# Ten outer products of tile 1's up stage in seven inner products each, with the weight sums read from three buffers

## The chip, the cores and the metric

The kernel runs on one core of a Trainium2 chip. A core has TensorE (matrix products, PE in the profile), VectorE (DVE), ScalarE (ACT), GpSimd (POOL) and SyncE (SP), each with a queue of its own that it works through in order, and DMA engines that move data between the core's memory (SBUF) and HBM. TensorE writes to PSUM; here PSUM holds four banks for products (bankA, bankB, bankC, bankE) and two areas for the attention. Transfers are started by an instruction in the queue of ScalarE or SyncE (ACTq, SPq), and whatever stands behind that instruction waits if it waits.

The metric is the device time of one execution in microseconds (us): before, the median of three runs is 1044.62 us (1042.49 to 1047.77).

## What is computed

A retention attention, whose output is the input of a SwiGLU feed-forward block; all in float32.

```python
scores = scale * np.matmul(q, k.transpose(0, 1, 3, 2))       # q, k, v: 8 x 8 heads x 576 x 64
Dmat = np.where(rel >= 0, gamma[:, None, None] ** rel[None, :, :], 0.0)
attn = np.matmul(scores * Dmat[None], v)
x = attn.transpose(0, 2, 1, 3).reshape(4608, 512)
g, val = x @ w_gate, x @ w_val                                # 512 x 1536 each
out = (g / (1 + exp(-g)) * val) @ w_out                       # 1536 x 512
```

## The kernel before

**Tiles and stages.** The 4608 tokens are worked in five tiles: tile 0 has 512 tokens, tiles 1 to 4 have 1024 each. The attention pairs of heads that a later tile needs are worked in small steps ("ticks") that are merged between the products of the tile before. Each of the tiles 1 to 4 has an up stage (gate and val products, SiLU and multiplication) and then a down stage.

**Sets.** The up stage of a tile multiplies in two levels, each a form of fast 2x2 block multiplication with seven products where eight are plain. The outer level makes seven sets, numbered 1 to 7, for each of three quarters of the hidden columns (`qd` 0 to 2); the order is `SETS = (1, 2, 6, 7, 4, 5, 3)` (line 109). A set has a 2x2 block of x and a 2x2 block of weights, for gate and val together. It is worked in one of two forms:

- *plain* (`PLAIN`, line 110): four output corners 11, 12, 21, 22, each the sum of two products, so eight slots (`whole_slot`, line 1220). A corner has one bank. When its second product is in, the bank is read once by VectorE (a 128x512 addition, `combine`), by ScalarE for set 1 (a copy), and twice by VectorE for set 5 (`whole_read`, line 1184).
- *seven inner products* (`slot`, line 1232): products 1, 5, 2, 6, 3 in the set's own slots, and 7 and 4 inside the next set's slots. Products 1, 6, 7, 4 go one after the other into one bank ("chain"), 5 and 3 into another ("side"), 2 into a third ("own"); between two products of a bank it is read (`first_read`, `second_read`), so there are seven reads instead of four. Products 1, 2, 3 use blocks of the weights as they are; products 7, 5, 6, 4 use the four *weight sums* 0, 1, 2, 3 of the set (`PLACE`, line 1043), and products 3, 5, 6, 7 use sums of x (`x_inner`, `view`).

A slot is two calls of `matmul` (gate, val) in `multiply` (line 1161); each call is two MATMUL records in the profile.

**Tile 1 before.** Tile 1 (called *busy* in the code) works all 21 sets in the plain form, 168 slots, straight from the weights in SBUF (`w_up`, the place `arena`). Meanwhile GpSimd makes for tiles 2 to 4 what they will read from HBM: for each quarter the weights of sets 5, 6, 7 and 4 (`outer_sums` in `w_sets`, eight 128x512 subtractions) and the four inner sums of all seven sets (`inner_sums`, four 128x256 subtractions for a set). Two buffers of 1024 columns hold the inner sums in turn; ScalarE's queue issues the transfers that store them (`store`, lines 1106 to 1110: the sums in one transfer of 512 KB, line 1109, the weights themselves in two of 256 KB, line 1110). A buffer is written again only when its store has landed.

**Order.** Every engine works in program order. `later(at, f)` puts an instruction ahead of slot `at`; `go` (line 1302) issues what is due, then the finished outputs that wait (`finish`, line 1171: SiLU on ScalarE into `io`, multiplication on VectorE, three slots after the output's last read), then the slot's matmuls and reads. Where a quarter begins is `begins[7 * qd]`: slots 0, 56 and 112. The first 56 slots run without ticks; over the rest six ticks are spread evenly.

```python
for i, o in enumerate(order):                       # order = (6, 4, 5, 7, 1, 2, 3)
    for j, f in enumerate(w_inner(o)):
        later(at + 8 + (13 * i + 3 * j) // 2, f)
    later(at + 8 + (13 * i + 9) // 2 + 6, *store(o, True))
```

## Time and profile before

| what | value |
|---|---|
| median of three runs | 1044.62 us |
| profiled execution, its own time | 1044.91 us |
| its span, first to last instruction | 1043.2 us |
| mean granted TensorE clock | 0.997 |
| TensorE busy | 1018.3 us (98%), 8380 matmul records |
| VectorE busy | 692.1 us (66%) |
| GpSimd busy | 551.0 us (53%) |
| ScalarE busy | 288.2 us (28%) |
| up stage of tile 1, first to last slot | 176.59 to 338.01 us of the span |

The times in the profile are counted from the first instruction. Busy shares are means over the whole span; what holds a stage is read from that stage. In the timeline, a line gives start, length, engine, line of the kernel, operation, output and inputs, and how often it follows itself; in brackets stands how long the engine had been idle before it, and what ended that. Matmuls overlap a little, so the time of a group of them is read from one start to the next.

### The profile page before, as it was taken

To read this page: it belongs to the slowest core of one execution; us is meant where nothing else is said; L and a number is where in the kernel's file an instruction comes from. 1 tells how busy PE (TensorE), PEld (TensorE's weight loads), DVE (VectorE), ACT (ScalarE), POOL (GpSimd) and SP (SyncE) were. 2 spreads that over 40 slices of the span, in tenths; PEclk is the share of its full clock that TensorE was granted. 3 is DMA by queue.
4 is the path that set the end of the run, shared out by engine and by line. 5 is a ranking of instruction groups with operands and counts; after the bars stand their busy time and mean duration, and the time that the engine had idled before them with its cause. 6 is when DMAs were issued, how large, how long until landed. Compare 5 with 4: busy or idle time off the path is not lost. (4 is left out here: it accounts for less than half of the span.)

```text
span 1043.2 us, 21372 instructions
## 1 busy us (share of the span) xinstructions
PE 1018.3 (98%) x8380; PEld 834.0 (80%) x8380; DVE 692.1 (66%) x1182; ACT 288.2 (28%) x638; POOL 551.0 (53%) x586
## 2 busy tenths in 40 slices
PE   6999999999999999999999999999999999999998
PEld 5655555888788888878888887888888888888887
DVE  4488883675857855875768777857576448566744
ACT  4466532131332321123332111133230012333110
POOL 3402263884635206854657237775582497566615
PEclk9999999999999999999999999999999999999999
DMA  9999887679485886756558767544454444445552
GB/s 241 253 273 240 213 226 252 204 190 253 134 244 156 224 240 198 198 170 172 177 157 242 202 169 203 168 148 142 142 190 152 154 157 150 169 141 176 185 159 96
DMA packets 292364, 197.13 MB, mean 189 GB/s; under 512 B 212968, under 2 KB 251112, under 8 KB 292264
## 3 DMA queue, kind: packets, MB, share of 16 engines
q10 hardware_dynamic: 58960, 121.12, 35.3%
q1 hardware_dynamic: 232664, 74.25, 29.9%
q8 instruction: 66, 1.08, 0.4%
q0 software_dynamic: 640, 0.39, 0.2%
...
## 5 line engine op out<-in xcount | busy, mean ns | idle before, releaser
L1041 POOL TENSOR_TENSOR rest<-rest 128x512 f32<-128x512 f32 (+1 forms) x147 | 155.6, 1073 | 158.6 <-DVE rest L1041 118.9
L1178 POOL TENSOR_TENSOR arena<-rest,io 128x256 f32<-128x256 f32 x144 | 105.4, 744 | 70.8 <-ACT io L1177 70.4
L1177 ACT ACTIVATE io<-rest 128x256 f32<-128x256 f32 x192 | 79.4, 417 | 225.1 <-DVE rest L1041 121.4
L1041 DVE TENSOR_TENSOR rest<-bankA,rest 128x512 f32<-128x512 f32 x100 | 67.7, 686 | 63.2 <-PE bankA L1163 46.2
L1163 PE MATMUL bankE<-rest,arena 128*128 128x256 f32 x424 | 108.0, 380 | 1.3 <-DVE rest L1041 1.2
L1163 PE MATMUL bankB<-rest,arena 128*128 128x256 f32 x416 | 106.4, 381 | 0.2
L1163 PE MATMUL bankA<-rest,arena 128*128 128x256 f32 x392 | 99.9, 381 | 1.4 <-DVE rest L1041 1.2
L1041 DVE TENSOR_TENSOR rest<-bankE,rest 128x512 f32<-128x512 f32 x108 | 73.0, 685 | 41.4 <-PE bankE L1163 23.8
L1041 DVE TENSOR_TENSOR rest<-bankC,rest 128x512 f32<-128x512 f32 x100 | 67.8, 685 | 44.0 <-PE bankC L1163 22.5
L1163 PE MATMUL bankC<-rest,arena 128*128 128x256 f32 x372 | 94.7, 381 | 0.6 <-DVE rest L1041 0.5
L1041 DVE TENSOR_TENSOR rest<-bankB,rest 128x512 f32<-128x512 f32 x101 | 68.7, 686 | 38.2 <-PE bankB L1163 25.0
L1163 PEld LDWEIGHTS bankE<-rest,arena 128*128 128x128 f32 x424 | 79.9, 190 | 14.1 <-DVE rest L1041 2.2
L1163 PEld LDWEIGHTS bankB<-rest,arena 128*128 128x128 f32 x416 | 78.2, 190 | 12.3 <-DVE rest L1041 1.1
L1163 PEld LDWEIGHTS bankA<-rest,arena 128*128 128x128 f32 x392 | 73.8, 190 | 13.6 <-DVE rest L1041 1.8
L1163 PEld LDWEIGHTS bankC<-rest,arena 128*128 128x128 f32 x372 | 69.8, 190 | 12.0 <-DVE rest L1041 2.5
L886 POOL TENSOR_TENSOR rest<-rest 128x256 f32<-128x256 f32 x43 | 35.4, 845 | 67.0 <-DVE rest L407 35.4
L1342 PE MATMUL bankE<-arena 128*128 128x256 f32 x264 | 61.0, 381 | 0.0
L1342 PE MATMUL bankC<-arena 128*128 128x256 f32 x264 | 60.8, 380 | 0.0
L1041 POOL TENSOR_TENSOR rest<-arena 128x256 f32<-128x256 f32 x42 | 31.5, 770 | 51.5 <-DMA up<-rest 51.5
L1342 PE MATMUL bankA<-arena 128*128 128x256 f32 x240 | 55.4, 380 | 1.8 <-POOL arena L886 1.8
L1342 PEld LDWEIGHTS bankC<-arena 128*128 128x128 f32 x264 | 50.0, 190 | 6.9
L1342 PEld LDWEIGHTS bankE<-arena 128*128 128x128 f32 x264 | 49.8, 190 | 6.9
...
## 6 DMA issues: line engine op xcount, KB each, us to landing
...
```

Source lines behind the costliest of these rows:

```text
L886: eng.tensor_tensor(out=dst, in0=srcs[0], in1=srcs[1], op=ALU.add if op[0] == "add" else ALU.subtract)
L1041: eng.tensor_tensor(out=out, in0=a, in1=b, op=ALU.add if sign > 0 else ALU.subtract)
L1163: m = nc.tensor.matmul(b[:, g * TB : (g + 1) * TB], w[:, g], x, start=(opens and g == 0), stop=True, skip_group_check=True)
L1177: nc.scalar.activation(out=s, in_=src[:, 0:TB], func=AF.Silu)
L1178: (nc.vector if busy else nc.gpsimd).tensor_tensor(out=hid[:, qd, 2 * H + h, 2 * T + t], in0=src[:, TB : 2 * TB], in1=s, op=ALU.mult)
L1342: nc.tensor.matmul(b[:, m * TB : (m + 1) * TB], lhs[:, qd, ts(m, P)], w[:, qd], start=(opens and qd == 0 and m == 0), stop=(qd == NQ - 1), ...
```

## The change

In tile 1, four sets of the seven in quarters 1 and 2 (6, 7, 4, 3) and two in quarter 0 (4, 3), ten in all, are worked in seven inner products instead of eight plain ones; sets 1, 2 and 5, and 6 and 7 of quarter 0, stay plain. That takes these parts:

- TensorE reads the weight sums for these sets from the buffers that GpSimd makes them in (`weights_of`: `new[o][:, :, at - 4]`). There are three buffers (`blocks`): 0 is in `rest`, 1 and 2 lie at the end of `arena`. Buffer 1 serves sets 6, 2, 5, buffer 2 serves 1, 4, and buffer 0 serves 7, 3.
- GpSimd's order in a quarter is another one: the outer sums of sets 5 and 6, the inner sums of 6, the outer sums of 7, the inner sums of 1, the outer sums of 4, and then the inner sums of 4, 7, 2, 5, 3 (in quarters 1 and 2 those of 7 ahead of 4). The stores of the sums stand at other slots: eight slots after the first sum of the set, for set 2 four.
- GpSimd also makes the inner sums of x for sets 4, 6, 3 and 7 (`x_inner`, sixteen 128x256 operations), in quarter 0.
- The first reads of sets 6, 7 and 4 in quarters 1 and 2 go by a ScalarE copy and a GpSimd addition, as they do in the later tiles (corner 12, and corner 22 of set 6, by VectorE).
- All sets share the four places of `ends`; a finished output that still waits is issued before its place is written again (`clear`). Corner 21 of set 4 has a place of its own. Corner 11 of set 5 is finished six slots on instead of three where the set before was in seven products.
- The operands of the first down steps are fetched at slots 45, 46 and 47 of quarter 2 instead of slots 120, 124 and 128.

Quarters now begin at slots 0, 52 and 104, and there are 158 slots. For each set the slots at which it starts within quarter 0 are 1: 0, 2: 8, 6: 16, 7: 24, 4: 32, 5: 37 and 3: 47; products 7 and 4 of set 4 stand at slots 39 and 43, those of set 3 at slots 2 and 6 of the next quarter.

```diff
--- before.py
+++ after.py
@@ -107,7 +107,7 @@
 
 
 SETS = (1, 2, 6, 7, 4, 5, 3)
-PLAIN = {(1, qd, o) for qd in range(3) for o in SETS}
+PLAIN = {(1, qd, o) for qd in range(3) for o in ((1, 2, 6, 7, 5) if qd == 0 else (1, 2, 5))}
 
 
 def terms(text):
@@ -1052,7 +1052,7 @@
         spots += [rest[:, sum_at + 1024 + TB * i : sum_at + 1024 + TB * (i + 1)] for i in range(2)]
         spots += [rest[:, dn_at + 4096 + TB * i : dn_at + 4096 + TB * (i + 1)] for i in range(12)]
         spots += [operands[:, 5376 + TB * i : 5376 + TB * (i + 1)] for i in range(3)]
-        new = {o: spots[3 * m : 3 * m + 3] for m, o in enumerate((1, 2, 7, 4, 5, 3, 6))}
+        new = {o: spots[3 * m : 3 * m + 3] for m, o in enumerate((1, 2, 7, 4, 6, 3, 5) if n == 1 else (1, 2, 7, 4, 5, 3, 6))}
         aside = new[3][2]
 
         def outer_sums(o, eng):
@@ -1083,13 +1083,15 @@
         first = x_inner(1, p) + x_outer(5, p) + x_outer(6, p)
         return first + x_outer(3, p) + x_inner(2, p) + x_outer(7, p) if n + 1 == NTILE else first
 
+    extra_at = lambda a, n: arena[:, 4 * QW + a : 4 * QW + a + n]
+
     def w_sets(qd):
 
         up = lambda n, k: w_up[:, qd, :, 2 * n : 2 * n + 2, k, :]
         sets = {1: up(0, 0), 2: up(0, 1), 7: up(1, 0), 3: up(1, 1), 5: hid[:, qd, 2:4, 0:2], 6: hid[:, qd, 0:2, 2:4], 4: hid[:, qd, 2:4, 2:4]}
-        new = [rest[:, a : a + 1024].rearrange("p (g j x) -> p g j x", g=2, j=4) for a in (x0_at + 1024, sum_at)]
+        blocks = (rest[:, x0_at + 1024 : x0_at + 2048], extra_at(1536, 1024), extra_at(0, 1024))
+        new = {o: blocks[b].rearrange("p (g j x) -> p g j x", g=2, j=4) for o, b in {6: 1, 1: 2, 7: 0, 4: 2, 2: 1, 5: 1, 3: 0}.items()}
         queue = nc.scalar
-        order = (6, 4, 5, 7, 1, 2, 3)
 
         def outer_sums(o):
             out, a, b = {5: (5, 7, 1), 6: (6, 3, 5), 7: (7, 3, 7), 4: (4, 2, 6)}[o]
@@ -1097,7 +1099,7 @@
 
         def inner_sums(o):
             z = lambda k, m: sets[o][:, :, m, k * P : (k + 1) * P]
-            to = lambda j: new[order.index(o) % 2][:, :, j]
+            to = lambda j: new[o][:, :, j]
             return [lambda: combine(nc.gpsimd, to(1), z(0, 1), z(0, 0), -1),
                     lambda: combine(nc.gpsimd, to(0), z(1, 1), z(0, 1), -1),
                     lambda: combine(nc.gpsimd, to(2), z(1, 1), to(1), -1),
@@ -1106,10 +1108,10 @@
         def store(o, new_ones):
             dst = up_sets[qd][SETS.index(o)].rearrange("p (g x) -> p g x", g=2)
             if new_ones:
-                return [lambda: queue.dma_start(out=dst[:, :, 512:1024], in_=new[order.index(o) % 2].rearrange("p g j x -> p g (j x)"))]
+                return [lambda: queue.dma_start(out=dst[:, :, 512:1024], in_=new[o].rearrange("p g j x -> p g (j x)"))]
             return [lambda m=m: queue.dma_start(out=dst[:, :, TB * (1 - m) : TB * (2 - m)], in_=sets[o][:, :, m]) for m in range(2)]
 
-        return sets, order, outer_sums, inner_sums, store
+        return sets, new, outer_sums, inner_sums, store
 
     def up_stage(n):
 
@@ -1125,7 +1127,7 @@
             held, ends, keep = place(0, 1, 2, 3), [place(4, 5, 6, 7)] * 2, place(8, 9, 10, 11)
         else:
             held, ends, keep = place(5, 6, 7, 10), [place(1, 3, 11, 8), place(0, 9, 2, 4)], None
-        number = {2: 0, 4: 1, 5: 0, 3: 1}
+        number = {2: 0, 4: 0, 5: 0, 3: 0} if busy else {2: 0, 4: 1, 5: 0, 3: 1}
         free = [banks[b] for b in rested] + ([inner[:, 0], outer[:, 0]] if n + 1 == NTILE else [])
         taken = {}
         waiting, after = [], {}
@@ -1143,6 +1145,8 @@
 
         def to(k, c):
             o = seq[k][1]
+            if busy and o == 4 and c == 21:
+                return rest[:, sum_at + 1024 : sum_at + 1536]
             return held[c] if o in (1, 6) else kept(k, c) if o == 7 else ends[number[o]][c]
 
         def addend(k, c):
@@ -1151,9 +1155,9 @@
         def weights_of(k):
             qd, o = seq[k]
             if busy:
-                sets = w_sets(qd)[0]
+                sets, new, *_ = w_sets(qd)
                 spot = [(kk, m) for m in (1, 0) for kk in range(2)]
-                return lambda at: sets[o][:, :, spot[at][1], spot[at][0] * P : (spot[at][0] + 1) * P]
+                return lambda at: sets[o][:, :, spot[at][1], spot[at][0] * P : (spot[at][0] + 1) * P] if at < 4 else new[o][:, :, at - 4]
             _, _, _, lo, width = fetches[base + k]
             w = operands[:, lo : lo + width].rearrange("p (g i x) -> p g i x", g=2, x=P)
             return lambda at: w[:, :, at if plain[k] else at - 1]
@@ -1179,10 +1183,18 @@
 
         def made(k, c, at):
             if seq[k][1] in final:
-                waiting.append((at + 3, k, c))
+                late = plain[k] and not plain[k - 1] and seq[k][1] == 5 and c == 11
+                waiting.append((at + (6 if late else 3), k, c))
+
+        def clear(k, c):
+            o = seq[k][1]
+            for e in [e for e in waiting if o in final and e[1] != k and e[2] == c and number[seq[e[1]][1]] == number[o]]:
+                waiting.remove(e)
+                finish(*e[1:])
 
         def whole_read(k, c, bank, at):
             o = seq[k][1]
+            clear(k, c)
             if o == 1:
                 nc.scalar.copy(out=to(k, c), in_=bank)
             elif o == 5:
@@ -1195,17 +1207,18 @@
         def first_read(k, c, bank):
             qd, o = seq[k]
             dst = to(k, c)
+            clear(k, c)
             if o == 1:
                 nc.scalar.copy(out=dst, in_=bank)
-            elif o == 5 and c != 12:
+            elif o == 5 and c != 12 and not busy:
                 nc.scalar.copy(out=dst, in_=bank)
                 combine(nc.gpsimd, held[c], held[c], dst, 1)
                 combine(nc.gpsimd, dst, dst, kept(k, c), 1)
             elif o == 5:
                 combine(nc.vector, held[c], bank, held[c], 1)
                 combine(nc.vector, dst, bank, kept(k, c), 1)
-            elif qd > 0 and o != 3 and c != 12:
-                t = ends[0 if o == 4 else 1][c]
+            elif qd > 0 and o != 3 and c != 12 and not (busy and (o, c) == (6, 22)):
+                t = dst if busy and o == 4 else ends[0 if o == 4 else 1][c]
                 nc.scalar.copy(out=t, in_=bank)
                 combine(nc.gpsimd, dst, t, addend(k, c), 1)
             else:
@@ -1286,15 +1299,19 @@
         else:
             for i, f in enumerate(x_outer(5, nc.vector) + x_outer(6, nc.vector) + x_outer(7, nc.vector) + x_outer(3, nc.vector)):
                 later(i if i < 4 else 2 * i + 2, f)
+            for o, at in {4: 16, 6: 32, 3: 36, 7: 47}.items():
+                for i, f in enumerate(x_inner(o, nc.gpsimd)):
+                    later(at + i, f)
             for qd in range(NQ):
                 at = begins[len(SETS) * qd]
-                _, order, w_outer, w_inner, store = w_sets(qd)
-                for i, f in enumerate([f for o in (5, 6, 7, 4) for f in w_outer(o)]):
-                    later(at + i, f)
-                for i, o in enumerate(order):
+                _, _, w_outer, w_inner, store = w_sets(qd)
+                for o, start in {5: 0, 6: 2, 7: 8, 4: 14}.items():
+                    for i, f in enumerate(w_outer(o)):
+                        later(at + start + i, f)
+                for o, start in {6: 4, 1: 10, 7: 24 if qd == 0 else 14, 4: 20, 2: 29, 5: 34, 3: 38}.items():
                     for j, f in enumerate(w_inner(o)):
-                        later(at + 8 + (13 * i + 3 * j) // 2, f)
-                    later(at + 8 + (13 * i + 9) // 2 + 6, *store(o, True))
+                        later(at + start + j, f)
+                    later(at + start + (4 if o == 2 else 8), *store(o, True))
                 for i, o in enumerate((1, 2, 6, 7, 4, 5, 3)):
                     for j, f in enumerate(store(o, False)):
                         later(at + 3 + 5 * i + 2 * j, f)
@@ -1309,7 +1326,7 @@
             after_tick()
             if at % (2 if busy else 3) == 1:
                 part_on()
-            if busy and at in (120, 124, 128):
+            if busy and at - begins[2 * len(SETS)] in (45, 46, 47):
                 fetch_one()
             if at + 1 == len(slots):
                 while waiting:
```

## The prediction

> **What bounds the kernel now.** I read the page's busy shares first, then the up stage of tile 1 by stretches (its quarters begin at 176.6, 225 and 273), then each engine's timeline in it.
>
> ```profile
> PE 1018.3 (98%) x8380; PEld 834.0 (80%) x8380; DVE 692.1 (66%) x1182; ACT 288.2 (28%) x638; POOL 551.0 (53%) x586
> 176.60:225.00 48.40, 48.37 (x224) 42.28 (x223) 30.77 (x45) 9.27 (x21) 35.34 (x38) 1.00 0.73 212
> 225.00:273.00 48.00, 48.00 (x410) 42.01 (x409) 29.30 (x56) 13.60 (x33) 28.59 (x36) 1.00 0.69 193
> 273.00:325.00 52.00, 49.90 (x597) 43.11 (x596) 30.79 (x59) 15.30 (x40) 24.61 (x28) 0.97 0.82 216
> ```
>
> In the last three rows the columns are length, then TensorE, weight loads, VectorE, ScalarE and GpSimd. TensorE is filled, so a matmul less is time less as long as nothing else takes the place; VectorE and GpSimd have a third of the stage free. The pitch of TensorE, and the one hole of the stage that counts:
>
> ```profile
> 190.40 1.89 PE L1163 MATMUL bankA<-rest,arena 128*128 128x256 f32 x8
> 192.13 1.89 PE L1163 MATMUL bankB<-rest,arena 128*128 128x256 f32 x8
> ...
> 279.40 0.52 PE L573 MATMUL inner<-qT,kT 64*64 64x64 f32 x21
> 282.02 0.35 PE L573 MATMUL inner<-qT,kT 64*64 64x64 f32 x9 [2.10 <-issue]
> 282.30 2.63 PE L1163 MATMUL bankA<-x_odd,arena 128*128 128x256 f32 x8
> 284.72 2.98 PE L1163 MATMUL bankB<-x_odd,arena 128*128 128x256 f32 x8
> 287.54 1.89 PE L1163 MATMUL bankC<-x_odd,arena 128*128 128x256 f32 x8
> ```
>
> Eight records take 192.13 - 190.40 = 1.73 us, so a slot of four takes 0.864 us; slot s of quarter 0 is due at 176.59 + 0.864 s. After a hole of 2.10 us two groups of eight take 5.24 us instead of 3.46 (the clock was halved): a hole of that size costs 1.8 us more than itself. GpSimd and ScalarE in quarter 0:
>
> ```profile
> 181.23 10.94 POOL L1041 TENSOR_TENSOR arena<-arena 128x512 f32<-128x512 f32 x8 [15.75 <-DMA out_dram<-arena]
> 192.13 2.04 POOL L1041 TENSOR_TENSOR rest<-arena 128x256 f32<-128x256 f32 x2
> 194.13 2.11 POOL L1041 TENSOR_TENSOR rest<-arena,rest 128x256 f32<-128x256 f32 x2
> 196.21 1.40 POOL L1041 TENSOR_TENSOR rest<-arena 128x256 f32<-128x256 f32 x2
> 197.57 1.59 POOL L1041 TENSOR_TENSOR rest<-arena,rest 128x256 f32<-128x256 f32 x2
> ...
> 196.27 0.52 ACTq L1109 DMA_DIRECT2D up<-rest  x1
> ...
> 197.51 0.42 ACT L1177 ACTIVATE io<-rest 128x256 f32<-128x256 f32 x1 [5.42 <-POOL rest L1041]
> ...
> 197.96 0.62 DVE L1178 TENSOR_TENSOR arena<-rest,io 128x256 f32<-128x256 f32 x1 [1.71 <-ACT io L1177]
> ```
>
> GpSimd starts at 181.23, held by tile 0's output; eight outer and eight inner sums are done at 197.57 + 1.59 = 199.2, four inner sums taking 3.0. The last three lines are the chain that I look for after the change: a store in ScalarE's queue waits for GpSimd's sums, a SiLU behind it waits 5.42 us, and VectorE stands behind its multiplication for 1.71 us with reads of banks queued. Here TensorE has banks enough not to notice.
>
> **What is removed.** Ten sets lose one slot each of eight: 10 x 0.864 = 8.6 us of TensorE. It has to come off the end, unless TensorE waits.
>
> **What is added.** Thirty bank reads; 16 sums of x on GpSimd (16 x 0.75 = 12 us, in quarter 0); ten copies on ScalarE and additions on GpSimd in quarters 1 and 2 (a 128x512 addition there is 1.37 by the row above); and waits of TensorE for sums just made. Seven reads with two slots or so between two products of one bank also leave VectorE less room to be late: a plain corner's bank is wanted again three corners (5 us) on, a chain or side bank three slots (2.6 us) on. The later fetch of the down operands (slots 45 to 47 of quarter 2, six to eight slots or 5 to 7 us ahead of the down stage) I cost at nothing, since such a fetch lands in 4.4 us by the page's issue list; if ScalarE issues it late, TensorE waits for the difference, 0 to 3 us, which goes into the range.
>
> **Quarter 0, GpSimd's clock.** Up to the sums of set 1 and the outer sums of set 4 GpSimd has the same sixteen operations as above, in another order: 199.2. Then x of set 4: 202.2; sums of 4: 205.2 (needed at slot 33, 205.1: nothing); sums of 7: 208.2; sums of 2 with one x operation between: 211.9. The store of set 2's sums stands at slot 33 of ScalarE's queue and so goes out at 211.9, with two weight stores of 0.63 behind it, then the SiLU of set 4's corner 11 (0.42): 214.1. VectorE's multiplication for it, at slot 37 (due 208.6), ends at 214.7. Behind it on VectorE: two reads of set 5's corner 11 (0.6 each, two take 1.29), a multiplication (0.6), the read of set 4's corner 22: 217.1. TensorE's product 4 of set 4, slot 43, goes into that bank and is due at 213.7. **First stall: 3.4 us**; slot 48 is now due at 221.4.
>
> The store of set 2 lands 3.3 us after its issue (median of its row), at 215.2, and only then may GpSimd write set 5's sums into the same buffer; with the x operations between it has seven to do: 220.4, and the first sum of set 3 at 221.9, all four at 224.9. Product 5 of set 3 (slot 48) waits 0.6. The store of set 5's sums (slot 42) has held ScalarE until 220.4, with four SiLUs behind it; four multiplications bring VectorE to 223.9, then two reads of corner 21 to 225.1: slot 49 waits 2.2. Two more reads, one multiplication that stands behind the store of set 3's sums (224.9 + 0.6 + 0.4 + 0.6), and the read of set 3's first product end at 227.5: slot 50 waits 1.5, slot 51 0.3. **Second stall: 4.6 us.** Quarter 0 gives back 8.0 of the 8.6. Ends: with GpSimd at the pace that it has where VectorE rests (1.28 for a large sum, alone at 272.88; 1.42 for two small ones at 199.40) the sixteen operations take 15.9 us instead of 18.0, and both stalls lose about 2: 4; with landings of 6.5 us, the longest of these stores' rows, 11.
>
> **Quarters 1 and 2, VectorE from set 5 to set 3.** Fifteen slots are 13.0 us of TensorE; a tick falls into them in both quarters (2.26 us, from 258.66 to 260.92). VectorE has in them 15 reads x 0.61 = 9.2, eight multiplications x 0.65 = 5.2, and the tick's own 4.0 (mask 0.6, states 2.0, two transpositions 1.4): 18.4 against 15.3. In the trace of before the same set 5 with a tick keeps VectorE busy from 265.14 to 281.79 and its last read (280.31) comes 2.6 us after its bank is full; plain sets follow and hide it. Now set 3 follows in seven products. I take the 3.1 with a little of the lag that no longer fits: **3.5 us in each quarter, 7.0.** The multiplications are the unsure term:
>
> ```profile
> L1178 DVE TENSOR_TENSOR arena<-rest,io 128x256 f32<-128x256 f32 x44 | 29.8, 678 | 7.2 <-ACT io L1177 7.2
> ```
>
> They mean 678 ns here, but 0.41 where GpSimd rests and 0.98 where it works: 1.1 us at the one end, 6 at the other, for each quarter; I take the mean since GpSimd makes sums all through this stretch. In quarters 1 and 2 GpSimd itself has 8 x 1.3 + 28 x 0.75 + 5 x 1.37 = 38 us for 52 slots and three ticks (some 51 us): no stall of its own in the likeliest case.
>
> **Sum.** -8.6 + 8.0 + 7.0 = +6.4 us against the profiled execution's 1044.9, which stands 0.3 over the median. The hole at 282.02 (2.10 + 1.8) may not come back in another program, and the first stall of 3.4 may halve the clock as that hole did (+1.8); I set these against each other. 1044.6 + 6.4 = 1051.0.
>
> The Trainium skill ("TensorE: Matmul & The Clock Gate", Part 1: The HAM clock gate) has the clock halved after an idle window of about 3.4 us. By that rule neither the 2.10 hole nor most of my stalls would cost anything beyond themselves, and the sum would stay 1051; by this case's row each stall of 2 us adds 1.8, and it would be 1053 to 1055. The row at 282.30 speaks against taking the rule as a threshold.
>
> **Rivals.**
> - *Faster: the lag never reaches TensorE.* The place is ScalarE's queue at slots 33 and 42. If GpSimd is done with set 2's sums 3.5 us earlier than I have it, the SiLU behind the store is in time, and with VectorE's lag held by the banks 2 us of stalls remain: 1044.6 - 8.6 + 2 = 1038. For it: no stall in this stage before although ScalarE was held 5.42 and 9.3 us. Against: GpSimd's start at 181.23 and its pace leave at most 2 us.
> - *A wash: quarter 0 as above, quarters 1 and 2 without stalls*, since banks absorb VectorE's 3.1: -8.6 + 8.0, 1044.
> - *Much slower: stores land late in quarters 1 and 2.* The sums of set 4 wait for the store of set 1's in the same buffer, and behind them in GpSimd's queue stand the additions of sets 7 and 4 that VectorE's second reads need. The waits for such stores before:
>
> ```profile
> POOL rest L1041 <- DMA up<-rest: 51.5, 13, 11.2
> ```
>
>  Four microseconds a wait on average and 11.2 at most, with nothing urgent behind them then. At 5 us more a quarter: 1061. It decides once a store lands over 4 us behind its slot.
>
> **How the numbers follow.** Likeliest (both kinds of stall) 0.45, its own range 1046 to 1056; faster 0.16; a wash 0.22; much slower 0.17. Range: from 1040 (between the faster case and the wash) to 1062. About 0.5% (5.2 us) is what a measurement of this kernel can tell from no change: slower than 1049.8 are the last rival and nine tenths of the likeliest, 0.58; within 0.5% the wash and a little of the likeliest, 0.25; faster 0.17.
>
> **What would show it.** TensorE's records of this stage fall by 80. Right: holes of TensorE near slots 43 and 48 to 51, put down to VectorE or GpSimd; SiLUs late behind the sums' stores; holes at set 3 of quarters 1 and 2. The steps are wrong if the stage has no holes over 0.5 us (then 8.6 us are gained), if set 2's sums end before 209, or if the holes sit at sets 7 and 4 of the later quarters. The whole is wrong if a later stage gives time back or takes it.

## The result and the profile after

Over six runs of each the kernel after takes 1055.24 us (median; 1052.82 to 1058.71) and the kernel before 1044.92 us (1039.45 to 1047.77): a ratio of 1.0107, 95% interval 1.0073 to 1.0140. It is slower by about 1%, 10.3 us by the medians; the forecast was 1051.0, so the sign holds and the time lies in the range that was given, 1040 to 1062, and the sum was 4 us short. The profiled execution took 1055.56 us (span 1053.8, mean granted clock 0.990; before 1044.91, 1043.2 and 0.997).

The line numbers move a little: TensorE's products are line 1167 now (1163 before), the stores of the sums 1111 and of the weights 1112, the SiLU 1181, its multiplication 1182. The page's busy shares of the kernel after:

```profile
PE 1016.7 (96%) x8340; PEld 828.3 (79%) x8340; DVE 698.4 (66%) x1203; ACT 292.9 (28%) x648; POOL 573.1 (54%) x612
```

TensorE has 40 records fewer (8380 before), which is ten slots of four, and is busy 1.6 us less, not 8.6. The up stage of tile 1 tells most of why. Here it is by its quarters (columns as in the prediction: length, then TensorE, weight loads, VectorE, ScalarE and GpSimd with their instructions, the granted clock, DMA):

```profile
174.60:232.50 57.90, 49.20 (x210) 40.51 (x209) 30.90 (x47) 7.90 (x18) 47.26 (x55) 0.95 0.65 193
232.50:290.10 57.60, 52.55 (x413) 44.54 (x412) 41.00 (x73) 18.48 (x43) 37.12 (x43) 0.94 0.64 177
290.10:350.50 60.40, 57.25 (x625) 48.67 (x624) 43.72 (x85) 21.50 (x53) 40.01 (x42) 0.96 0.77 208
```

The stage takes 175.9 us against 161.4 before (quarters 48.6, 57.1, 55.7), though it has ten slots fewer: the removed slots are gone (8.6 us), and 23 us of new loss stand against them. That is 14.5 us more, where the two executions differ by 10.6: the kernel after came to this stage 2.0 us earlier (174.6 and 176.6 us of the span) and needed 1.9 us less behind it (703.3 and 705.2). Both parts differ from execution to execution: over the profiles of this document the stage begins at 171.5 to 183.8 us, and what follows it takes 702.8 to 706.1. Whether any of the 3.9 us comes from the change is not shown. So the whole loss lies in this stage, and the stage shows it better than the time of a single execution. TensorE's waits over the stage in the kernel after, by what ended them (total, times, longest):

```profile
PE bankC L1167 <- DVE rest L1041: 4.6, 3, 2.3
PE bankB L1167 <- DVE rest L1041: 4.4, 3, 2.9
PE bankA L1167 <- DVE rest L1041: 3.8, 3, 1.9
PE bankE L1167 <- DVE rest L1041: 2.7, 3, 1.2
PE bankA L1167 <- POOL rest L1041: 1.4, 1, 1.4
```

That is 16.9 us; before it was one wait of 2.1 for "issue" and one of 0.4 for VectorE. Nearly all of it is a bank that VectorE has not read yet. For quarter 0, here are TensorE, then ScalarE, VectorE and GpSimd in the timeline of the kernel after:

```profile
216.40 1.10 PE L1167 MATMUL bankA<-x_odd,arena 128*128 128x256 f32 x4 [1.94 <-DVE rest L1041]
...
222.31 1.13 PE L1167 MATMUL bankA<-rest 128*128 128x256 f32 x4 [1.35 <-POOL rest L1041]
226.39 1.88 PE L1167 MATMUL bankB<-rest,arena 128*128 128x256 f32 x4 [2.95 <-DVE rest L1041]
228.92 1.62 PE L1167 MATMUL bankC<-rest 128*128 128x256 f32 x3 [0.66 <-DVE rest L1041]
...
210.82 0.52 ACTq L1111 DMA_DIRECT2D up<-arena  x1
211.38 1.71 ACTq L1112 DMA_DIRECT2D up<-arena  x2
213.19 0.72 ACT L1181 ACTIVATE io<-rest 128x256 f32<-128x256 f32 x2 [15.37 <-DMA kn<-in_k_dram]
220.92 0.52 ACTq L1111 DMA_DIRECT2D up<-arena  x1
221.54 1.34 ACT L1181 ACTIVATE io<-rest 128x256 f32<-128x256 f32 x4 [7.63 <-POOL arena L1041]
...
213.70 0.42 DVE L1182 TENSOR_TENSOR arena<-rest,io 128x256 f32<-128x256 f32 x1 [3.68 <-ACT io L1181]
...
222.05 3.09 DVE L1182 TENSOR_TENSOR arena<-rest,io 128x256 f32<-128x256 f32 x4 [3.81 <-ACT io L1181]
225.06 1.28 DVE L1041 TENSOR_TENSOR rest<-bankB,rest 128x512 f32<-128x512 f32 x2
...
216.05 0.73 POOL L1041 TENSOR_TENSOR arena<-arena 128x256 f32<-128x256 f32 x1 [3.89 <-DMA up<-arena]
```

Read from below: the store of set 2's sums goes out at 210.82, and only when it has landed, at 216.05, does GpSimd write set 5's sums; the next store, 220.92, waits for these. Each time the SiLUs stand in ScalarE's queue behind a store that waits for GpSimd (213.19, 221.54), VectorE waits for them for 3.68 and 3.81 us, and the bank reads are behind that. (The bracket at 213.19 names an old transfer: issuing a store isn't counted as busy. What ScalarE stood at is the store just above.) In the quarters behind, this is set 5 to set 3 of quarter 1, VectorE and then TensorE:

```profile
274.32 1.45 DVE L1182 TENSOR_TENSOR arena<-rest,io 128x256 f32<-128x256 f32 x1 [1.63 <-ACT io L1181]
...
279.94 1.42 DVE L1182 TENSOR_TENSOR arena<-rest,io 128x256 f32<-128x256 f32 x4
281.28 1.28 DVE L1041 TENSOR_TENSOR rest<-bankB,rest 128x512 f32<-128x512 f32 x2
...
276.43 1.13 PE L1167 MATMUL bankC<-x_odd,arena 128*128 128x256 f32 x4 [2.34 <-DVE rest L1041]
...
278.67 3.16 PE L1167 MATMUL bankA<-rest,arena 128*128 128x256 f32 x8
...
285.50 1.10 PE L1167 MATMUL bankE<-rest 128*128 128x256 f32 x4 [1.07 <-DVE rest L1041]
288.24 2.08 PE L1167 MATMUL bankC<-rest,arena 128*128 128x256 f32 x4 [1.64 <-DVE rest L1041]
```

VectorE works without a pause from 274.32 to 289.4, TensorE waits three times for it, and after the wait of 2.34 eight records take 3.00 us (278.67 to 281.67) where 1.73 is usual. The granted clock (the last column but two) in the stretches behind such waits:

```profile
226.60:233.40 6.80, 6.14 (x15) 4.38 (x15) 5.18 (x10) 1.08 (x3) 6.80 (x7) 0.50 0.39 111
277.80:281.20 3.40, 3.40 (x9) 2.65 (x9) 3.33 (x10) 0.83 (x2) 0.00 (x0) 0.50 0.06 22
288.10:291.50 3.40, 3.26 (x8) 2.63 (x9) 2.31 (x5) 0.42 (x1) 1.82 (x2) 0.50 0.80 129
346.10:349.50 3.40, 3.26 (x8) 2.64 (x9) 2.30 (x5) 0.78 (x2) 2.76 (x2) 0.50 0.57 93
214.50:222.00 7.50, 4.55 (x20) 3.72 (x20) 3.64 (x7) 0.46 (x2) 5.95 (x9) 1.00 0.72 160
```

Half clock for 17 us of the stage, worth 8.5 us of TensorE's work at most (before: one stretch of 3.4 us at 283.5). That is why TensorE is as busy in the stage as before (159.0 and 158.9 us) with 8.6 us of products less: the 13.6 us of half clock that are new make up for 6.8 of it. The last row is the wait of 1.94 at slot 43, after which the clock stayed whole.

To compare the runs I use one number for a quarter: its *loss*, the sum over its slots of what each takes above 0.8635 us, where that is over 0.15. The ticks' own work is in it: 10.7 us in quarters 1 and 2 together, before and after alike. Each row is one profiled execution; the ratios are over all runs, each against the kernel before on the same chip. Five of the runs, e1, e3, e4, f3 and g5, compute the same as the kernel after. The others multiply wrong operands in places, as is told with each; they serve to show what holds the time and are no kernels to use.

| kernel | loss of quarters 0, 1, 2 (us) | up stage (us) | ratio to before, 95% interval |
|---|---|---|---|
| before | 0.2, 8.3, 6.9 | 161.4 | 1 |
| after | 12.6, 12.4, 13.5 | 175.9 | 1.0107 [1.0073, 1.0140] |
| e1_sums_store_on_sync | 17.1, 17.4, 22.3 | 194.3 | 1.0324 [1.0273, 1.0374] |
| e2_fourth_buffer | 9.1, 11.3, 13.7 | 171.5 | 1.0090 [1.0063, 1.0118] |
| e3_ticks_moved | 12.1, 8.7, 13.9 | 172.6 | 1.0083 [1.0060, 1.0106] |
| e4_kept_warm | 12.5, 11.3, 14.4 | 175.9 | 1.0102 [1.0062, 1.0142] |
| f1_late_stores | 4.1, 11.1, 11.7 | 164.7 | 1.0085 [1.0060, 1.0111] |
| f2_sums_in_time | 5.5, 14.2, 11.6 | 169.1 | 1.0074 [1.0050, 1.0098] |
| f3_mult_on_gpsimd | 11.2, 6.0, 8.0 | 162.5 | 1.0019 [0.9993, 1.0045] |
| f4_all | 3.0, 5.7, 10.2 | 156.8 | 0.9999 [0.9972, 1.0027] |
| g1_order_and_mult | 2.5, 9.3, 8.0 | 157.4 | 0.9984 [0.9961, 1.0007] |
| g2_with_ticks | 2.6, 9.6, 12.3 | 162.2 | 1.0021 [0.9995, 1.0048] |
| g3_order_and_mult | 4.5, 6.4, 8.0 | 156.4 | 0.9955 [0.9927, 0.9982] |
| g5_order_and_mult | 2.7, 11.8, 8.5 | 160.2 | 0.9987 [0.9959, 1.0016] |

One thing bears on quarter 0 that no edit set. GpSimd stands for 16 to 19 us before its first sums of the stage, and counted from the stage's first slot it begins them at another time in each execution: 6.1 us in the kernel after, 3.7 in e2, 4.1 in f1, 8.4 in e4. Where it begins later, whatever waits for its sums is later.

### The profile page after: what moved, and what is told of

The parts are those of the page before. It is cut to its first block, busy times and chain, and to the rows that moved or that the text cites. A ratio compares the mean times of both kernels' runs of the same rounds, so it can differ in the third digit from the quotient of the medians.

```text
span 1053.8 us, 21402 instructions
## 1 busy us (share of the span) xinstructions
PE 1016.7 (96%) x8340; PEld 828.3 (79%) x8340; DVE 698.4 (66%) x1203; ACT 292.9 (28%) x648; POOL 573.1 (54%) x612
## 5 line engine op out<-in xcount | busy, mean ns | idle before, releaser
L1041 POOL TENSOR_TENSOR rest<-rest 128x512 f32<-128x512 f32 (+1 forms) x165 | 174.4, 1071 | 173.2 <-DVE rest L1041 119.6
L1167 PE MATMUL bankC<-rest,arena 128*128 128x256 f32 x412 | 106.7, 383 | 2.6 <-DVE rest L1041 2.4
L1041 DVE TENSOR_TENSOR rest<-bankC,rest 128x512 f32<-128x512 f32 x115 | 77.8, 685 | 43.3 <-PE bankC L1167 21.9
L1041 POOL TENSOR_TENSOR arena<-arena 128x256 f32<-128x256 f32 (+1 forms) x84 | 75.9, 925 | 39.5 <-ACT rest L1199 16.2
L1167 PE MATMUL bankA<-rest,arena 128*128 128x256 f32 x352 | 92.8, 388 | 0.6 <-DVE rest L1041 0.5
L1167 PEld LDWEIGHTS bankC<-rest,arena 128*128 128x128 f32 x412 | 78.1, 191 | 14.8 <-DVE rest L1041 3.0
L1167 PEld LDWEIGHTS bankE<-rest,arena 128*128 128x128 f32 x396 | 74.9, 191 | 14.2 <-DVE rest L1041 3.5
L1167 PEld LDWEIGHTS bankA<-rest,arena 128*128 128x128 f32 x352 | 67.5, 194 | 12.5 <-DVE rest L1041 2.5
L1359 PE MATMUL bankA<-arena 128*128 128x256 f32 x264 | 60.8, 380 | 0.0
L1359 PE MATMUL bankB<-arena 128*128 128x256 f32 x240 | 55.4, 380 | 1.8 <-POOL arena L886 1.8
L1359 PEld LDWEIGHTS bankA<-arena 128*128 128x128 f32 x264 | 50.0, 190 | 6.8
```

Of the source, the lines that this page charges most:

```text
L1041: eng.tensor_tensor(out=out, in0=a, in1=b, op=ALU.add if sign > 0 else ALU.subtract)
L1167: m = nc.tensor.matmul(b[:, g * TB : (g + 1) * TB], w[:, g], x, start=(opens and g == 0), stop=True, skip_group_check=True)
L1359: nc.tensor.matmul(b[:, m * TB : (m + 1) * TB], lhs[:, qd, ts(m, P)], w[:, qd], start=(opens and qd == 0 and m == 0), stop=(qd == NQ - 1), ...
```

## Experiments on quarter 0, the ticks and the clock

All of them start from the kernel after. **The stores of the sums on SyncE's queue**, so that ScalarE's SiLUs stand behind none of them:

```diff
 def store(o, new_ones):
     if new_ones:
-        return [lambda: queue.dma_start(out=dst[:, :, 512:1024], ...)]
+        return [lambda: nc.sync.dma_start(out=dst[:, :, 512:1024], ...)]
```

> One edit: the stores of the inner weight sums are issued by SyncE's queue instead of ScalarE's. Theory S (ScalarE stands at a store until GpSimd has made the sums, the SiLUs behind it are late, VectorE stands at their multiplications and does not free banks): in quarter 0 the holes near 194, 198, 214, 223 and 228 us (0.39, 1.26, 1.94, 2.95, 0.66) go, and one hole at the first sum of set 3 stays, 2 to 5 us, since GpSimd is as late as before; the half clock of 6.8 us after 226 shrinks to 3.4 or goes; 5 to 9 us less than the changed kernel (1046 to 1050, ratio to the kernel before about 1.003). Rival (GpSimd's lateness alone sets when set 3 can go on, ScalarE only follows it): the holes move together into one at set 3 of quarter 0 and the time stays within 2 us of 1055.

Measured: 1078.53 us, the slowest of all. The waits of GpSimd and of SyncE's queue in this kernel's stage (total, times, longest):

```profile
POOL arena L1041 <- DMA up<-arena: 46.2, 6, 10.7
...
SPq L1111 <- POOL arena L1041: 49.3, 7, 11.0
```

A store now stands in a queue with the attention's loads (line 282, which wait for VectorE), goes out late and lands late; GpSimd, which may not write the buffer before, waits 46.2 us instead of 10.5, and TensorE twice over 6 us for sums (6.73 at 202.1, 6.42 at 224.0). The holes at 194 and 198 us are gone, as theory S had it. So the run does not show that ScalarE's queue was innocent: it shows that the wait is bound to the store and goes where the store goes, and that three buffers leave a store no time to be late.

**A fourth buffer for set 5's sums**, so that GpSimd needn't wait for the landing of set 2's store:

```diff
-blocks = (rest[:, x0_at + 1024 : x0_at + 2048], extra_at(1536, 1024), extra_at(0, 1024))
+blocks = (..., rest[:, sum_at : sum_at + 1024])
-{6: 1, 1: 2, 7: 0, 4: 2, 2: 1, 5: 1, 3: 0}
+{6: 1, 1: 2, 7: 0, 4: 2, 2: 1, 5: 3, 3: 0}
```

The place is taken by sums of x of sets 3 and 6, which set 5's sums overwrite, here and in f1, f2 and f4: some products of tile 1 then have other operands, and GpSimd waits for TensorE's reads there.

> One edit: the sums of set 5 are made in a fourth buffer (1024 columns of rest at sum_at) instead of in buffer 1 behind set 2's sums. Theory B (GpSimd waits for the store of set 2, 3.89 us in quarter 0, and everything up to set 3's sums is late by that): the wait goes, the first sum of set 3 is there at about 218.5 instead of 222.3, the store of set 5 goes out near 217 instead of 220.9; the holes at 220.96, 223.44 and 228.26 (5.0 us together) shrink to 1 to 2 us, the one at 214.46 (1.94, behind the store of set 2's sums) stays; with the half clock of 6.8 us gone 5 to 7 us less, 1048 to 1050. Rival (VectorE has simply too much to do from set 5 to set 3, as in the later quarters): the holes at slots 49 to 51 stay at 3 us or more, and the time is 1052 to 1055.

Measured: 1053.34 us over eight executions, one of which took 2134 us (1052.77 without it); the ratio, 1.0090, lies within the interval of the kernel after. TensorE in this kernel at slots 43 and 49 to 50, and ScalarE's queue ahead of slot 49:

```profile
218.06 1.10 PE L1167 MATMUL bankA<-x_odd,arena 128*128 128x256 f32 x4 [2.66 <-DVE rest L1041]
...
226.26 1.26 PE L1167 MATMUL bankB<-rest,arena 128*128 128x256 f32 x4 [2.77 <-DVE rest L1041]
228.53 2.04 PE L1167 MATMUL bankC<-rest 128*128 128x256 f32 x4 [1.01 <-DVE rest L1041]
...
220.78 0.55 ACTq L1111 DMA_DIRECT2D up<-rest  x1
221.44 1.34 ACT L1181 ACTIVATE io<-rest 128x256 f32<-128x256 f32 x4 [6.51 <-POOL rest L1041]
```

The wait for the sum itself (1.35 at 220.96 in the kernel after) is gone, the one of 2.95 behind it is still 2.77. But the run does not take away what it was to take away: the store of set 5's sums goes out at 220.78 instead of near 217, though the sums are ready at 218.70, and hardly earlier than in the kernel after (220.92). It seems to wait for a sum of x (ended at 220.75) that goes to the same place. The four SiLUs behind it come at 221.44 as before (221.54), and VectorE waits 2.05 us for them. So this run shows that the lateness of set 3's sum is not what holds slot 49; whether the store in ScalarE's queue does, f1 below tells. Of the 3.5 us that quarter 0 loses less here, 2.1 are at slots 21 to 25, where no store was moved: GpSimd began earlier in this execution.

**The ticks of quarters 1 and 2 at other slots**, out of set 5 to set 3: they go in ahead of the slots 56 + (0, 10, 22, 51, 61, 74).

> One edit: the six attention ticks of tile 1's up stage stand at slots 56, 66, 78, 107, 117 and 130 instead of 56, 73, 90, 107, 124 and 141, so that none falls into sets 5 and 3 of quarters 1 and 2. Theory V (VectorE is overloaded there by 18.4 us of work in 15.3 us because of the tick): the holes of quarters 1 and 2 (2.34, 1.07, 1.64, 1.75, 1.23: 8.0 us) shrink to 2 us or less in all, and with them three of the half clock stretches (10.2 us, 5.1 us lost): 7 to 11 us less, 1044 to 1048. Rival (ScalarE held by the stores makes VectorE late there too, tick or not): the holes of these quarters stay above 5 us, and the time is within 3 us of 1055.

Measured: 1051.48 us, ratio 1.0083: 3.8 us less than the kernel after by the medians, where 7 to 11 were expected, and the intervals overlap. In the profile the holes of these quarters sum to 6.4 us instead of 8.0, and 3.4 us of their 10.2 at half clock are left. Without the ticks' own work quarter 1's loss falls from 8.8 to 5.1; at sets 5 and 3 it falls from 8.3 to 3.1, and 1.4 are new at slots 75 and 79. Quarter 2's is 6.8 instead of 6.4: at set 3 it falls from 5.5 to 4.2, and 1.9 are new at slots 124 to 127, as in every run with the ticks moved (f4, g2). So the tick was most of what quarter 1 lost there and a quarter of what quarter 2 lost there, and part of it only moves.

**TensorE kept busy over the holes of quarter 0** by small products into a PSUM area that nobody reads then:

```diff
+for _ in range({43: 8, 48: 4, 49: 12}.get(at, 0) if busy else 0):
+    nc.tensor.matmul(outer[:, 1, 0:P], ident, ident, start=True, stop=True, skip_group_check=True)
```

> One edit that adds work: 8, 4 and 12 small matmul calls (128x128 of the identity by itself, into a part of PSUM that the attention does not use in quarter 0) ahead of slots 43, 48 and 49 of quarter 0, about 0.2 us each, to fill the holes of 1.94, 1.35 and 2.95 us. Theory C (the holes themselves make the clock halve, which costs half of the stretch on top): the 6.8 us of half clock after 226 us go, the slots of sets 3 and 1 run at 0.86 us again, and the time is 3 us less, about 1052, although 24 calls are added. Rival (the clock is halved by something else, or the waits behind are VectorE's anyway and swallow it): no change, or longer by what the calls take beyond the holes, 1055 to 1057.

Measured: 1054.24 us. TensorE in this kernel (line 1325 is the filler):

```profile
222.58 2.84 PE L1325 MATMUL outer<-ident 128*128 128x128 f32 x24
...
227.75 1.10 PE L1167 MATMUL bankC<-rest 128*128 128x256 f32 x4 [1.41 <-DVE rest L1041]
```

The clock stays whole in quarter 0 (1.00, where the kernel after has 0.95 there), and the quarter is no shorter: 58.0 us against 57.9, loss 12.5 against 12.6. But the sum hides two things. Slot 50, which waited 0.66 behind slow products, now waits 1.41 behind fast ones: there a faster TensorE only comes earlier to the next bank that is not read. Behind it nothing waits, and slots 50 to 52 lose 0.2 us instead of 2.3. Against that this execution has a hole of 1.8 us at 189 that the kernel after hasn't: GpSimd began 8.4 us after the first slot, and VectorE waited 5.16 us for a SiLU. So of the 3.4 us that 6.8 us at half clock can cost, some 2 were gained and 0.75 were swallowed by VectorE's lateness; four executions can't tell 2 us from nothing.

**The stores later in ScalarE's queue**, with the fourth buffer, so that they stand behind the SiLUs (quarter 0: set 6 at slot 19, 1 at 19, 7 at 32, 4 at 28, 2 at 45, 5 at 50, 3 at 55; in the others set 6 at 12, 1 at 18, 7 at 22, in quarter 2 set 2 at 38), and **the sums of set 3 ahead of those of set 5 as well**:

```diff
-later(at + start + (4 if o == 2 else 8), *store(o, True))
+later(at + when[o], *store(o, True))                # f1, f2
-{4: 16, 6: 32, 3: 36, 7: 47}                        # sums of x
+{4: 16, 3: 32, 6: 43, 7: 47}                        # f2
-2: 29, 5: 34, 3: 38
+2: 29, 3: 35, 5: 39                                 # f2
```

> Set 5's sums in a fourth buffer, and the stores of the sums stay in ScalarE's queue but stand where no SiLU that is due waits behind them (quarter 0: sets 6 and 1 at slot 19, 2 at 45, 5 at 50, 3 at 55). GpSimd's order is that of the changed kernel. Theory S (ScalarE held by stores): the time that quarter 0's slots lose beyond 0.86 us each, 12.6 us in the changed kernel, falls to 4 or less, what stays being the first sum of set 3 that comes late (slot 48, 2 to 3 us); 1046 to 1049. Rival (VectorE's amount of work from set 5 to set 3): quarter 0 still loses 8 us or more, near slots 48 to 51, and the time is 1052 to 1054.

> As the run with late stores, and GpSimd makes the sums of set 3 (and of its x) ahead of those of set 5, which TensorE does not read in tile 1. Theory S and B together: quarter 0 loses 1.5 us or less beyond its slots, and 1 to 3 us less in quarters 1 and 2, 1044 to 1047, about the kernel before. If quarter 0 still loses over 4 us with the first sum of set 3 in time, neither the stores nor the sums were its cause, and VectorE's work is.

Measured: 1052.01 us for both, beside 1043.36 for before. TensorE in f1 at slots 49 and 50, and at the end of quarter 2; then that end in the kernel after:

```profile
222.60 1.13 PE L1167 MATMUL bankB<-rest,arena 128*128 128x256 f32 x4 [0.35 <-DVE rest L1041]
225.14 1.10 PE L1167 MATMUL bankC<-rest 128*128 128x256 f32 x4 [1.41 <-DVE rest L1041]
...
337.38 1.10 PE L1167 MATMUL bankA<-rest 128*128 128x256 f32 x4 [1.75 <-DVE rest L1041]
339.71 1.13 PE L1167 MATMUL bankE<-rest,arena 128*128 128x256 f32 x4 [1.23 <-DVE rest L1041]
```

```profile
343.90 1.10 PE L1167 MATMUL bankA<-rest 128*128 128x256 f32 x4 [1.75 <-DVE rest L1041]
346.24 2.07 PE L1167 MATMUL bankE<-rest,arena 128*128 128x256 f32 x4 [1.23 <-DVE rest L1041]
```

f1 differs from e2 by the places of the stores alone, and GpSimd begins at nearly the same time in both. Slot 49 waits 0.35 instead of 2.77, and quarter 0's loss falls from 9.1 to 4.1 (f2: 5.5): the store in ScalarE's queue, with the SiLUs behind it, is what held slot 49 in e2, and the same rows (221.54, 222.05, 226.39) stand in the kernel after. Over all runs f1 is not faster than e2 all the same (1.0085 against 1.0090). f1's profiled execution took 1048.40, 3.6 less than its median, so its row flatters it. With quarters 1 and 2 as they are, this order is worth 1 to 2 us by the ratios, which the intervals can't tell from nothing. The stores of quarters 1 and 2 were moved too, and these quarters lose 11.1 and 11.7 instead of 11.3 and 13.7.

The last four lines settle another point. The same two waits, 1.75 and 1.23, were followed by half clock in the kernel after (2.07 us for four records) and by whole clock in f1 (1.13). From the first of the two slots to the end of the stage f1 takes 5.4 us, the kernel after 6.6, and e2, which has the same two waits and 6.8 us at half clock, 7.6. So at this place 3.4 us at half clock cost 1.3 us, and 6.8 cost 2.3.

## Experiments on VectorE's load, and a better order

**The multiplications of sets 4 and 5 on GpSimd in quarters 1 and 2**, and nothing else:

```diff
 def finish(k, c):
-    (nc.vector if busy else nc.gpsimd).tensor_tensor(out=hid[...], in0=..., in1=s, op=ALU.mult)
+    (nc.vector if busy and not (qd > 0 and o in (4, 5)) else nc.gpsimd).tensor_tensor(...)
```

> One edit to the changed kernel: the multiplications that finish sets 4 and 5 in quarters 1 and 2 are made by GpSimd instead of VectorE (sixteen of 0.4 to 1.4 us). Theory V (from set 5 to set 3 VectorE has more work than the slots have time): the 8.8 and 6.4 us that quarters 1 and 2 lose beyond slots and ticks fall to 4 and 3 or less, and the time by 6 to 9 us with the clock, 1046 to 1049; quarter 0 is as it was. Rival (what these quarters lose comes from ScalarE's and GpSimd's lateness): they lose as much as now or more, since GpSimd gets 6 us more to do in each: 1054 to 1060.

Measured: 1044.60 us, ratio 1.0019. One condition takes 16 multiplications from VectorE and gets back 0.9% of the time. Quarters 1 and 2 of this kernel, and the moved operation in them (duration in ns, least, median, most):

```profile
231.50:282.60 51.10, 49.58 (x413) 42.76 (x412) 36.48 (x65) 18.06 (x43) 40.53 (x49) 0.99 0.68 193
282.60:337.70 55.10, 54.84 (x626) 47.17 (x626) 41.05 (x76) 21.65 (x54) 44.21 (x51) 1.00 0.83 224
```

```profile
L1182 DVE TENSOR_TENSOR arena<-rest,io x17: 398/720/1330, 232.3 to 336.5; 128x256 f32<-128x256 f32 x17
L1182 POOL TENSOR_TENSOR arena<-rest,io x16: 726/730/744, 269.5 to 333.1; 128x256 f32<-128x256 f32 x16
```

Against the kernel after VectorE is busy 4.5 and 2.7 us less in the two quarters, and they are 6.5 and 5.3 us shorter. Without the ticks' work the loss falls from 8.8 and 6.4 to 2.3 and 0.9, and only one stretch of half clock, that of quarter 0, is left in the stage. The cause of most of what quarters 1 and 2 lose is shown by this: the multiplications in VectorE's queue between set 5 and set 3. What it doesn't separate is their own time from what VectorE stands still ahead of them. The multiplication at 274.32 in the kernel after had waited 1.63 us for its SiLU, which stood in ScalarE's queue behind the tick's copies, and the hole of 2.34 follows it; f3 takes both from VectorE. The stores are not the cause here: f1 moved them, and these quarters lose about as much.

**All of it together**: fourth buffer, later stores, set 3's sums first, moved ticks, multiplications on GpSimd.

> Late stores, fourth buffer, set 3's sums ahead of set 5's, the multiplications of sets 4 and 5 of quarters 1 and 2 on GpSimd, and the ticks of these quarters moved off sets 5 and 3. If the three causes (stores in ScalarE's queue, order of GpSimd's sums, VectorE's work at set 5) hold all of the 23 us that tile 1's slots lose more than before, this gains most of the 8.6 us that the ten slots are worth: 1036 to 1041. If some 5 us or more are still lost in the stage, another cause is open: 1042 to 1047.

Measured: 1043.40 us, ratio 0.9999. The stage is 4.6 us shorter than before in the profile (156.8), the time over all runs is the same. (The profiled execution, 1048.43, is 5 us above the median; it came to the stage at 183.8 us, the latest of all.)

**A new order of quarter 0 with the three buffers.** With the multiplications on GpSimd, its sums are made in the order 6, 1, 4, 3, 7, 2, 5: those that TensorE reads first; set 3's get a buffer of their own, and the stores go behind the SiLUs of the set in work. g2 has the ticks of e3 in addition.

```diff
-{6: 1, 1: 2, 7: 0, 4: 2, 2: 1, 5: 1, 3: 0}                       # buffers
+{6: 1, 1: 2, 4: 1, 3: 0, 7: 2, 2: 1, 5: 2}                       # quarter 0
-{6: 4, 1: 10, 7: 24, 4: 20, 2: 29, 5: 34, 3: 38}                 # first sum at slot
+{6: 4, 1: 10, 4: 22, 3: 37, 7: 41, 2: 46, 5: 50}
-{4: 16, 6: 32, 3: 36, 7: 47}                                     # sums of x
+{4: 18, 3: 33, 6: 45, 7: 49}
-later(at + start + (4 if o == 2 else 8), *store(o, True))
+later(at + {6: 19, 1: 21, 4: 40, 3: 46, 7: 47, 2: 54, 5: 60}[o], *store(o, True))
```

In quarter 1 the three buffers change places (6, 2 and 5 in buffer 0, 1 and 4 in 1, 7 and 3 in 2), and set 6's sums stand at its slot 7 instead of 4; quarter 2 is as it was. In both runs the last sums of set 5 in quarter 0 are made from places that have been written over.

> The multiplications of sets 4 and 5 of quarters 1 and 2 are on GpSimd, and quarter 0 is put into another order with the same three buffers: GpSimd makes the sums that TensorE reads (sets 4 and 3) before those that are only stored (7, 2, 5), set 3's sums get a buffer of their own that nothing has to leave first, and the stores of the sums stand behind the SiLUs of the set in work instead of ahead of them. Theory Q (quarter 0's 8 to 9 us at slots 42 to 51 and the 2 us at slots 21 to 25 come from the order of queues alone, not from the amount of work): quarter 0's loss falls from 11.2 us to about 4, set 3's sums are done by 212 us of the span, the up stage takes 155 us, the time is 1037 us (1034 to 1040), ratio 0.993 to 0.996. Rival W (GpSimd has 44 us of work in a quarter of 45, and VectorE its reads and multiplications: whatever the order, somebody is late): quarter 0 loses 8 us or more, time 1042 to 1046. A part of W would be that the sums now made last come late for quarter 1: holes of TensorE at its slots 17 to 25 (set 6), 2 to 4 us, time 1040.

> As the run before it, and the ticks of quarters 1 and 2 moved out of the slots between set 5 and set 3. Theory V (VectorE's work from set 5 to set 3 is what quarters 1 and 2 lose, and with the multiplications gone it fits): there is little left to gain; loss without the ticks' own work falls from 2.3 to 1 us in quarter 1 and stays under 1 in quarter 2, time 1 to 2 us below the run before, 1035 to 1036. Rival (the ticks still collide with the last reads): 3 to 4 us below it, 1033.

Measured: g1 1037.16 us beside 1039.81 for before on this chip, ratio 0.9984; g2 1042.24, ratio 1.0021: neither differs from before beyond its interval. Quarter 0's loss is 2.5 us, as the theory has it, and 3.8 come back at slots 57 to 60, where VectorE's first finish of set 3 waits 3.21 us for the last sum of set 5. The moved ticks, worth 2 to 4 us to the kernel after, cost 5 here: quarter 2 loses 12.3 instead of 8.0, with waits for GpSimd that g1 hasn't (0.9 us in quarter 1, 1.3 in quarter 2). So what a place of the ticks is worth is not a figure of its own; it seems to depend on which engine has room there.

**The same, with set 5's sums directly after set 3's:**

```diff
-{6: 4, 1: 10, 4: 22, 3: 37, 7: 41, 2: 46, 5: 50}
+{6: 4, 1: 10, 4: 22, 3: 37, 5: 41, 7: 45, 2: 53}
-{6: 19, 1: 21, 4: 40, 3: 46, 7: 47, 2: 54, 5: 60}
+{6: 19, 1: 21, 4: 40, 3: 46, 5: 47, 7: 54, 2: 62}
-{4: 18, 3: 33, 6: 45, 7: 49}                                     # sums of x
+{4: 18, 3: 33, 6: 49, 7: 54}
```

> As g1_order_and_mult, but set 5's sums of quarter 0 are made directly after set 3's (they read a place that the finish of set 3's outputs writes), and those of sets 7 and 2 and the sums of x of sets 6 and 7 after them; the ticks are where the change has them. In g1 VectorE's first finish of set 3 waited 3.21 us for set 5's last sum on GpSimd, TensorE had a hole of 1.89 us at 224.33, the clock fell for 3.4 us behind it, and slots 57 to 60 lost 3.8 us. Theory Q: with this order that wait is gone, quarter 0 loses 2.5 us as in g1, quarter 1 9.3 - 3.8 = 5.5, quarter 2 8.0: 16 us in all, as much as before loses (15.5), so that the 8.6 us of the removed slots come through less half a microsecond: the up stage takes 153.5 us, the time is 8 us under the kernel before of the same chip, ratio 0.990 to 0.994. Rival W (what is moved comes late somewhere else: the sums of 7 and 2 and of x now run into quarter 1, where GpSimd also has the outer sums and the multiplications): a new hole of 2 to 4 us at slots 60 to 80, ratio 0.996 to 0.999.

Measured: 1038.12 us beside 1042.22, ratio 0.9955 [0.9927, 0.9982]: faster than before by 0.45%, in the stage 5.0 us. (Set 2's last sums of quarter 0 are made from places written over, as the next expectation tells. No run with the sums as they should be is faster than before.) The holes at slots 57 to 60 are gone as expected (quarter 1's loss 9.3 to 6.4), quarter 0 loses 4.5 instead of 2.5.

**And with the store of set 5's sums behind the SiLUs, set 2's sums ahead of quarter 1's outer sums:**

```diff
-{6: 4, 1: 10, 4: 22, 3: 37, 5: 41, 7: 45, 2: 53}
+{6: 4, 1: 10, 4: 22, 3: 36, 5: 40, 7: 44, 2: 52}
-{6: 19, 1: 21, 4: 40, 3: 46, 5: 47, 7: 54, 2: 62}
+{6: 19, 1: 21, 4: 40, 3: 50, 5: 52, 7: 57, 2: 62}
-{5: 0, 6: 2, 7: 8, 4: 14}                                        # outer sums
+{5: 4, 6: 6, 7: 8, 4: 14}                                        # quarter 1
-{4: 18, 3: 33, 6: 49, 7: 54}                                     # sums of x
+{4: 18, 3: 33, 6: 44, 7: 46}
```

> The order of g3_order_and_mult with two more steps. One: quarter 0's sums of set 2 are made while their weights still stand (in g1 the last sums of set 5, and in g3 those of set 2, were made from places that had been written over; that moves no time, but those two compute other sums there than the kernel after). Two: the store of set 5's sums moves from slot 47 to slot 52, that of set 3's from 46 to 50, and the sums of x of sets 6 and 7 come before set 2's sums. In g3 ScalarE stood 3.77 us at the store of set 5's sums with the SiLUs of slot 48 behind it, VectorE's multiplication and the reads of banks behind those, and TensorE lost 4.5 us at slots 48 to 51. Theory Q (the order of ScalarE's queue): these SiLUs now go out in time, quarter 0's loss falls from 4.5 to 1 to 2 us, quarters 1 and 2 stay at 6.4 and 8.0, the up stage takes 153.5 us (g3 156.4, before 161.4), ratio to before 0.992 to 0.995. Rival W (VectorE's four multiplications at 0.95 us in a row beside GpSimd are what holds the banks): the loss stays at 4 us or more, ratio 0.995 to 0.998; or the sums for set 6 of quarter 1, one slot nearer to their use, come late: a hole near slot 71.

Measured: 1040.73 us beside 1042.51, ratio 0.9987 [0.9959, 1.0016]: no difference from before. VectorE ahead of slot 49, in g3 and then in g5:

```profile
216.25 3.08 DVE L1182 TENSOR_TENSOR arena<-rest,io 128x256 f32<-128x256 f32 x4
219.25 1.27 DVE L1041 TENSOR_TENSOR rest<-bankB,rest 128x512 f32<-128x512 f32 x2
```

```profile
210.87 3.23 DVE L1182 TENSOR_TENSOR arena<-rest,io 128x256 f32<-128x256 f32 x4
214.02 1.27 DVE L1041 TENSOR_TENSOR rest<-bankB,rest 128x512 f32<-128x512 f32 x2
...
244.97 0.69 DVE L1041 TENSOR_TENSOR rest<-bankA,rest 128x512 f32<-128x512 f32 x1 [3.32 <-POOL rest L1041]
```

The first two lines of each are alike: four multiplications in a row, 3.1 to 3.2 us, and then the reads that free the bank of slot 48. They are there with the store in front of the SiLUs and without, and slots 48 and 49 lose 2.9 and 2.5 us. So what is left in quarter 0 is not the store that I blamed, and the multiplications (rival W) are what the rows show in its place. The last line is the price of the other step: GpSimd has ten small sums in a row (8.71 us from 235.01), the addition for a bank read of set 6 comes behind them at 243.68, VectorE waits 3.32 and TensorE 3.16 us for it, and slots 72 to 78 lose 7.5 us, 1.3 of which is the tick that is always there.

## Why the prediction was right, and where it was off

**What is removed: right.** Ten slots of 0.864. The records fall by 40, not by 80 as I wrote at the end: a slot has four records, and I had counted eight.

**Quarter 0: the chain is right, link by link; the sum was 4.6 short.** Store of set 2's sums 210.82 (predicted 211.9), SiLU 213.19 to 213.91 (its end predicted 214.1), slot 43 at 216.40 (217.1); set 5's first sum 216.05 (215.2), its store 220.92 (220.4), set 3's first sum 222.26 (221.9), slot 49 at 226.39 (225.1). The holes of the quarter sum to 8.55 us against 8.0. That these times agree to about a microsecond is partly luck: the stage began 2.0 us earlier than in the profile that the prediction was reckoned from, so each of them stands for 2 us more of TensorE's time. Before slot 43 it lost 4.4 us, not 3.4, and from slot 47 on 8.2, not 4.6. Two things were not in the sum. The stores of sets 6 and 1 stand ahead of set 2's SiLUs (189.44 and 196.17), and VectorE's waits behind them cost 2.3 us at slots 21 to 25; I had looked for the chain at the two stores at slots 33 and 42 only, though the trace of before showed it at such a store, as a wait that cost nothing. And the products behind the second stall ran at half clock.

ScalarE's store is a link that is shown. f1, with the stores behind the SiLUs, has 0.35 us at slot 49 where e2 has 2.77. The holes at slots 21 to 25 are gone in every run with such stores (f1, f2, f4, g1, g2, g3, g5), also where GpSimd begins as late as in the kernel after (f2 7.6 us, g1 6.2, g5 6.5). Between the landing of set 2's store and slot 49 the link is not tested alone, since in e2 the next store was as late as ever. What is left at slots 47 to 51 in f1, g3 and g5 (2.9, 4.5 and 2.7 us) has no late store ahead of it; four multiplications of VectorE stand there in a row, and they didn't wait for a SiLU. That these are the cause is read from the rows; no run takes them away.

**Quarters 1 and 2: right as to the engine and the place, and shown by f3.** Predicted 7.0 us for VectorE's overload; the holes are 5.05 and 2.98, 8.0 in all, and by loss, with the half clock in it, the quarters have 10.6 us more than before. One step was too even: I had the tick as the same part of the overload in both quarters, and by e3 it was most of it in the first and a quarter in the second.

**The term that was mis-sized: the clock.** I set the hole of before (2.10 + 1.8) against one halving (+1.8), a net of nothing. The hole did not come back, as I thought it might not; but the stage has five windows of half clock for before's one, 17 us for 3.4. Counted as holes, the prediction has 15.0 us of new ones and the profile 16.6 (those over 0.25 us); by loss the quarters have 23.1 more than before. So the stage was 8 us worse than forecast, and the total only 4, because the rest of the kernel was 3.9 us shorter, for which the prediction has no term: that part of the agreement is luck. What the half clock costs by itself is less than half of its length wherever a run shows it: some 2 us for 6.8 in quarter 0 (e4), 1.3 for 3.4 and 2.3 for 6.8 at the end of quarter 2 (the kernel after and e2 beside f1). In quarter 1 no run took the clock's part away alone, so its share there stays open.

The prediction weighed a rule of the Trainium skill ("TensorE: Matmul & The Clock Gate", Part 1: The HAM clock gate), half clock after an idle window of about 3.4 us, against the row at 282.30, and took the row. The runs side with the row: waits of 2.34 us, or 1.75 and 1.23 close together, were followed by 3.4 us at half clock. But the row gives no threshold either, since the wait of 1.94 us at slot 43 was followed by none (last row of the clock's windows), and the same 1.75 and 1.23 were followed by none in f1. The same section says that the window runs freely; stretches of 3.4 and 6.8 us agree with that, and so do their beginnings in the kernel after, which lie 51.2, 10.2 and 58.0 us apart, 15, 3 and 17 times 3.41. That the same waits fall differently into such windows would explain why they halve the clock in one execution and not in another; no run here shows which share of a window decides.

**The rivals.** *Faster, the lag never reaches TensorE*: it does, 13 times by the waits shown above, 12 of them for VectorE. *A wash, quarters 1 and 2 without stalls*: no, 8.0 us of holes; f3 makes such a time of the kernel (1.0019), by one line. *Much slower, stores land late in quarters 1 and 2*: GpSimd waited 10.5 us in four waits for landings over the stage, the longest 3.89, and no hole sits at sets 7 and 4; e1 shows what that rival would have looked like. The later fetch of the down operands cost nothing: the down stage's first product follows with no wait.
